# Values of two query chunks taken together in the second half of an attention kernel, with four tiles of transposed weights

## The chip, the cores and the metric

The kernel runs on one core of one Trainium2 chip. The core has five engines that run their own instruction streams in order and wait for each other by semaphores: TensorE (PE, matmuls; its weight loads are shown as PEld), VectorE (DVE), ScalarE (ACT), GpSimd (POOL) and SyncE (SP), which here only issues DMA transfers. Tiles live in SBUF (128 partitions) or PSUM (128 partitions, in banks of 512 float32, where matmuls put their results). The metric is the device time of one execution in microseconds (us); less is better. Runs of the kernel before: a median of 807.25 us of 3 (806.58 to 809.42).

## The reference

An attention of B = 4 batches, H = 8 heads, S = 576 positions and D = 64, with a bias that a small network of one hidden layer computes from the logarithm of the distance, and behind it an MLP with a squared ReLU on the 2304 tokens of 512 features:

```python
scores = scale * np.matmul(q, k.transpose(0, 1, 3, 2)) + bias
scores = scores - np.max(scores, axis=-1, keepdims=True)
attn = np.exp(scores)
attn = attn / (np.sum(attn, axis=-1, keepdims=True) + 1e-09)
x = np.matmul(attn, v)           # (B, H, S, D), then laid out as (B*S, H*D)
h = x @ w_in                     # 512 -> 2048
r = np.maximum(h, 0.0)
out = (r * r) @ w_out            # 2048 -> 512
```

## The kernel before, in words

The attention is cut into 80 units. A unit is one batch, one pair of heads (`hp`) and one chunk of queries (`ic`): four chunks of 128 queries and one last chunk (`TAIL`) of 64, in which both heads share one tile. Units 0 to 39 are batches 0 and 1; for them the bias is built beside the attention. Units 40 to 79 are batches 2 and 3, with the five chunks of one head pair in a row (`NA` = 40 is the border). This second half is where the change is.

A unit goes through three stages, each of them one or two units behind the one before in the loop over `s`:

- `scores(s)`: four matmuls (L428) into the tile `sp`, which is four banks of PSUM and exists once. DVE adds the bias and takes the row's maximum (L434, once for each head: the instructions `t,negm`, with a small one that reads `negm`), and ACT takes the exponential into `p` and the sums into `sums` (L439).
- `transposes(s - 2)`: PE transposes `p` into the PSUM tiles `pp` (eight 128x128 blocks, L477) and `pa` (the last keys of both heads, L480), and ACT copies them to the SBUF tile `pt` (L478, L481). There are two `pt` tiles, in the pool `att`.
- `values(s - 3)`: ten matmuls (L495) of `pt` with the values into the PSUM tile `px`, and one copy of `px` into the transposed output `xT` (L500), on DVE from unit 4 on.

When a head pair of a batch is complete, `normalise` (L448, L449) and `scale_x` multiply its part of `xT` by the inverse sums, which PE spreads over the partitions (`ra`, `rt`, L456, L463; DVE L466). All of `pp`, `pa`, `px`, `ra`, `rt` take turns in four banks with the tag `aux`.

Keys and queries of the second half come by SyncE's queue (L137 to L151) into the pool `kqb`, which takes the space of the first half's pool `kqa`, so that the first of these transfers waits for the last scores of unit 39. Behind them on the same queue come the weights. `load_w` (L172) brings 512 KB of `w_in` into one of two `stage` tiles, and `scan_w` takes its largest magnitude on DVE (L189, 16 scans from loop turn `SC` = 41 on, kept in the program's order). Once all 16 are through, one common scale is worked out (L215 to L218, and a matmul `pw`), and from turn `WB` = 53 on twelve of the weights are loaded again and split into two float16 parts (`split_in`): ACT takes a magnitude (L180), DVE works on the one tile `zw` (L183 to L186), POOL forms sums and differences (L238 to L240), ACT writes the high part (L227) and DVE the low part (L228) into `area`. The same four DVE operations on a tile `wa` begin the conversion of a weight of `w_out`; the first of these stand at the end of the attention, and more run in the MLP. The MLP's first matmuls (`ha`, L704) need the last `xT` of the batches, by way of the DVE multiplication L466 of the last head pair.

Nobody writes down the order of an engine's instructions: tiles are taken in turn from their pools, and a scheduler that simulates the engines' times sets the order in which each engine runs. The scans and the score matmuls are kept in program order. Where a change alters tiles or instructions, the order of others can change with it. These line numbers are those of the kernel before; in the kernel after, the value copy is L508, and L478, L481 and L495 are L479, L482 and L502.

Of the kernel before, what the change touches and what calls it, by code (L numbers as in the profile page):

```python
# [10 lines left out]
F32 = mybir.dt.float32  # L11
# [19 lines left out]
TAIL = 4  # L31
# [48 lines left out]
def attention_then_relu2_mlp(ctx: ExitStack, tc: tile.TileContext, q, k, v, cols, w_in, w_out, psi, xmat, dist, out):  # L80
    nc = tc.nc
    PE, DVE, ACT, POOL, SP = nc.tensor, nc.vector, nc.scalar, nc.gpsimd, nc.sync
# [5 lines left out]
    att = att_stack.enter_context(tc.tile_pool(name="att", bufs=1, side="right"))  # L88
# [37 lines left out]
    NA = len(units)  # L126
    units += [(b, hp, ic) for hp in range(HP) for b in range(AB, B) for ic in range(NIC)]
    NU = len(units)
    k1_t, v_t, q_t = {}, {}, {}
# [338 lines left out]
    def transposes(u):  # L468
        n = 2 if units[u][2] < TAIL else 1
        p = p_t.pop(u)  # L470
        b, hp, ic = units[u]
        pt = att.tile([128, 9, 128], F32, name="pt", tag="pt", bufs=2)
        for h in range(n):
            pp = ps.tile([128, 512], F32, name="pp", tag="aux", bufs=4)
            for c in range(4):
                k0 = h * (S + 64) + 128 * c
                PE.transpose(pp[:, 128 * c:128 * c + 128], p[:, k0:k0 + 128], ident)  # L477
            ACT.copy(pt[:, 4 * h:4 * h + 4], pp.rearrange("p (c m) -> p c m", c=4))  # L478
        pa = ps.tile([128, 512], F32, name="pa", tag="aux", bufs=4)  # L479
        PE.transpose(pa[:, :128], p[:, S - 64:S + 64], ident)  # L480
        ACT.copy(pt[:, 8], pa[:, :128])  # L481
        pt_t[u] = pt  # L482

    def values(u):
        b, hp, ic = units[u]
        pt, vt = pt_t.pop(u), v_t[b, hp]
        w = 64 if ic == TAIL else 128
        px = ps.tile([128, 512], F32, name="px", tag="aux", bufs=4)
        for c in range(5):
            for h in range(2):  # L490
                if c == 4:
                    src = pt[:, 8, 64 * h:64 * h + 64] if ic == TAIL else pt[:, 8, :w]
                else:
                    src = pt[:, c, 64 * h:64 * h + 64] if ic == TAIL else pt[:, 4 * h + c, :w]
                PE.matmul(px[64 * h:64 * h + 64, :w], lhsT=vt[:, c, h], rhs=src, start=(c == 0), stop=(c == 4))  # L495
        end = S if ic == TAIL else 128 * ic + 128
        if u < XC:
            ACT.copy(xT[b][:, hp, end - w:end], px[:, :w])
        else:
            DVE.tensor_copy(out=xT[b][:, hp, end - w:end], in_=px[:, :w])  # L500
# [376 lines left out]
```

## Time and profile before

One execution was recorded by the profiler. It took 803.41 us; its span from first to last instruction is 801.6 us.

| | us |
|---|---|
| median of 3 runs | 807.25 |
| profiled execution | 803.41 |
| span of it | 801.6 |
| PE busy | 731.9 (91%) |
| DVE busy | 546.0 (68%) |
| ACT busy | 453.8 (57%) |
| POOL busy | 272.8 (34%) |

The time is that of the whole program, and busy times are sums over it. The stages differ: the first half of the attention ends at about 208 us, the weights' scans at about 270, the attention at 402.7, and the MLP takes the rest. In a row of the timeline the last part in square brackets is the time for which the engine stood idle before it, and what it waited for; `x20` says that a row stands for 20 instructions. A float32 matmul of the program shows as two in the trace.

### The profile page before, as it was taken

What the parts mean: (1) busy time and instruction counts of PE and PEld (TensorE: products, weight loads), DVE (VectorE), ACT (ScalarE), POOL (GpSimd) and SP (SyncE); (2) the same over time, 40 slices, a digit from 0 to 9 for tenths busy, and PEclk for the clock granted to TensorE, in tenths of its full rate; (3) what the DMA queues carried; (4) which work ended last, traced back from release to release, by engine and by line L of the source; (5) the groups of instructions that cost most, each with busy time, mean ns of one, the idle gap of its engine ahead of it and who ended that gap; (6) DMA issues with size and microseconds to landing.
All of it is one profiled execution on the core that took longest, in us unless ns stands there. A gap on an engine that the chain in (4) does not pass through costs nothing.

```text
span 801.6 us, 17870 instructions
## 1 busy us (share of the span) xinstructions
PE 731.9 (91%) x7238; PEld 583.4 (73%) x7238; DVE 546.0 (68%) x1135; ACT 453.8 (57%) x924; POOL 272.8 (34%) x292
## 2 busy tenths in 40 slices
PE   6499999999988898988999899989999999999992
PEld 5457787777766676666678677767888888888881
DVE  7877888875457778887888968785654466445541
ACT  5767787777645468786865555575642233224320
POOL 1454323340001012141266645745451244223320
PEclk7979999999999999999999999999999999999997
DMA  7610000000475422211221132102020001000100
GB/s 207 188 57 17 3 16 3 2 3 5 125 276 196 159 81 88 84 54 54 80 90 70 66 119 104 55 1 79 1 79 1 1 1 54 1 1 2 53 2 26
DMA packets 27990, 50.14 MB, mean 63 GB/s; under 512 B 5252, under 2 KB 13444, under 8 KB 27908
## 3 DMA queue, kind: packets, MB, share of 16 engines
q1 hardware_dynamic: 27908, 49.01, 18.6%
q8 instruction: 57, 0.93, 0.5%
q14 instruction: 25, 0.20, 0.1%
HBM read 43.23 MB, written 5.77 MB: 61 GB/s over the span
## 4 chain that ended last, share of the span: by engine, by line
PE 53%; DVE 17%; ACT 8%; DMA 7%; issue 7%; POOL 4%; SPq 2%; POOLq 0%; DVEq 0%; ACTq 0%
PE y L753 16%; PE sp L428 8%; PE px L495 7%; PE ha L704 7%; PE hb L704 6%; PE pp L477 5%; DMA stage<-in_w_in 4%; PE bb L383 4%; DVE t L434 2%; ACT p L439 2%; DVE area L605 2%; ACT pt L478 1%; DVE zw L185 1%; DVE area L228 1%; DVE small L189 1%
## 5 line engine op out<-in xcount | busy, mean ns | idle before, releaser
L753 PE MATMUL y<-w,gh 128*128 128x512 f32 x576 | 176.7, 401 | 2.6 <-ACT gh L733 2.4
L704 PEld LDWEIGHTS <-area 128*128 128x128 f16 x1680 | 148.1, 99 | 42.2 <-issue 17.6
L439 ACT ACTIVATE p<-t,negm 128x576 f32<-128x576 f32 x144 | 111.4, 776 | 27.3 <-DVE negm L434 27.1
L434 DVE CUSTOM_DVE_ANT_0 t<-sp,area 128x576 f32<-128x576 f32 x144 | 104.0, 753 | 29.9 <-PE sp L428 24.8
L753 PEld LDWEIGHTS y<-w,gh 128*128 128x128 f32 x576 | 105.1, 190 | 23.9 <-ACT gh L733 3.8
L428 PE MATMUL sp<-k,q 64*128 64x288 f32 (+1 forms) x640 | 105.3, 441 | 15.4 <-DVE negm L434 7.6
L495 PE MATMUL px<-pt,v 128*64 128x128 f32 (+1 forms) x1600 | 99.2, 272 | 7.5 <-DVE xT L500 2.8
L753 PE MATMUL y<-w,gl 128*128 128x512 f32 x288 | 106.0, 395 | 0.0
L704 PE MATMUL ha<-area 128*128 128x256 f16 (+1 forms) x960 | 105.2, 263 | 0.5 <-DVE xT L466 0.5
L478 ACT COPY pt<-pp 128x512 f32<-128x512 f32 x144 | 80.4, 583 | 41.5 <-PE pp L477 41.4
L495 PEld LDWEIGHTS px<-pt,v 128*64 128x64 f32 x1600 | 81.5, 139 | 24.2 <-issue 9.5
L704 PE MATMUL hb<-area 128*128 128x256 f16 (+1 forms) x720 | 83.9, 270 | 8.0 <-DVE area L723 4.7
L477 PE MATMUL pp<-ident,p 128*128 128x128 f32 x576 | 84.7, 283 | 3.3 <-ACT p L439 2.5
L428 PEld LDWEIGHTS sp<-k,q 64*128 64x128 f32 (+1 forms) x640 | 55.2, 179 | 39.7 <-issue 14.0
L398 POOL TENSOR_TENSOR area<-bt,bt 128x256 f32<-128x256 f32 x72 | 53.5, 768 | 80.6 <-DVE bt L393 80.6
L477 PEld LDWEIGHTS pp<-ident,p 128*128 128x128 f32 x576 | 62.2, 142 | 21.3 <-issue 8.4
L383 PE MATMUL bb<-wmov,mask 128*128 128x64 f16 x1440 | 51.2, 197 | 13.7 <-DVE bt L404 11.0
L753 PEld LDWEIGHTS y<-w,gl 128*128 128x128 f32 x288 | 53.7, 188 | 11.9 <-DVE gl L734 0.7
L383 PEld LDWEIGHTS <-mask 128*128 128x128 f16 x1440 | 46.9, 100 | 20.7 <-DVE bt L404 11.8
L719 POOL TENSOR_TENSOR area<-area 128x512 f32<-128x512 f32 (+1 forms) x20 | 24.3, 1215 | 92.8 <-ACT area L718 83.9
L369 DVE TENSOR_TENSOR mask<-sdist,theta 128x1024 f16<-128x1024 f16 (+1 forms) x78 | 50.3, 677 | 7.9 <-PE bb L383 7.9
L733 ACT CAST gh<-area 128x512 fp32r<-128x512 f32 (+1 forms) x40 | 22.2, 574 | 44.0 <-DVE area L728 32.9
(146 smaller groups left out, 1024.2 us busy)
## 6 DMA issues: line engine op xcount, KB each, us to landing
stage<-in_w_in SPq DMA_DIRECT2D x32, 512.0 KB, 3.7
stage<-in_w_out SPq DMA_DIRECT2D x16, 512.0 KB, 3.5
v<-in_v SPq DMA_DIRECT2D x16, 320.0 KB, 3.7
out<-o SPq DMA_DIRECT2D x18, 256.0 KB, 2.0
q<-in_q SPq DMA_DIRECT2D x32, 128.0 KB, 2.9
k<-in_k SPq DMA_DIRECT2D x16, 160.0 KB, 3.5
k<-in_k SPq DMA_DIRECT2D x16, 144.0 KB, 3.5
xc<-in_xmat SPq DMA_DIRECT2D x5, 288.0 KB, 3.3
```

The source lines that it names most:

```text
L369: DVE.tensor_tensor(out=m[:, :, :w], in0=win, in1=th.to_broadcast([128, 8, w]), op=ALU.is_ge)
L383: PE.matmul(bb[:, 64 * (7 - r):64 * (8 - r)], lhsT=m[:, r], rhs=wmov[:, n], start=(n == 0), stop=(n == 1))
L398: POOL.tensor_tensor(out=dst, in0=tw, in1=sw, op=ALU.add)
L428: mm = PE.matmul(out_t[to, x, :HALF], lhsT=qt[rows, cols], rhs=kt[rows, k0:k0 + HALF], start=True, stop=True)
L434: DVE.tensor_tensor_reduce(out=t.rearrange("p (x n) -> p x n", x=2), in0=sp[:, :, :HALF], in1=bias.rearrange("p (x n) -> p x n", x=2), sca ...
L439: ACT.activation(out=p[:, S * n:S * n + S], in_=t, func=AF.Exp, bias=negm[:, n:n + 1], scale=-1.0, accum_out=sums[:, 2 * ic + n:2 * ic + n ...
L477: PE.transpose(pp[:, 128 * c:128 * c + 128], p[:, k0:k0 + 128], ident)
L478: ACT.copy(pt[:, 4 * h:4 * h + 4], pp.rearrange("p (c m) -> p c m", c=4))
L495: PE.matmul(px[64 * h:64 * h + 64, :w], lhsT=vt[:, c, h], rhs=src, start=(c == 0), stop=(c == 4))
L704: PE.matmul(h[:, s, :w], lhsT=a, rhs=x, start=(k == 0), stop=(k == 5))
L719: POOL.tensor_tensor(out=c[:, 2:4], in0=s[:, 1:3], in1=s[:, 0:4:3], op=ALU.subtract)
L753: PE.matmul(y, lhsT=a[:, slot, o:o + 128], rhs=x, start=((n, P) in firsts and f == 0 and m == 0), stop=((n, P) in lasts and f == 1 and m = ...
```

## The change

In units 40 to 79 the values of the chunks 0 and 1, and of 2 and 3, are taken together: for the first of a pair nothing is done, and for the second 20 matmuls are made, 128 columns of `px` for each unit, with one copy of 256 columns. The tail stays alone. To keep two units' transposed weights for that, `pt` tiles of the second half alternate, two units at a time, between the two tiles in `att` and two more in the pool `kqb`. A `pt` tile takes 4,608 bytes of a partition, so that 9,216 more are taken in `kqb`, and keys and queries lie elsewhere in it.

```diff
--- before.py
+++ after.py
@@ -469,7 +469,8 @@
         n = 2 if units[u][2] < TAIL else 1
         p = p_t.pop(u)
         b, hp, ic = units[u]
-        pt = att.tile([128, 9, 128], F32, name="pt", tag="pt", bufs=2)
+        pool = kq_p[-1] if u >= NA and u // 2 % 2 else att
+        pt = pool.tile([128, 9, 128], F32, name="pt", tag="pt", bufs=2)
         for h in range(n):
             pp = ps.tile([128, 512], F32, name="pp", tag="aux", bufs=4)
             for c in range(4):
@@ -482,17 +483,24 @@
         pt_t[u] = pt
 
     def values(u):
+
         b, hp, ic = units[u]
-        pt, vt = pt_t.pop(u), v_t[b, hp]
+        if u >= NA and ic in (0, 2):
+            return
+        vt = v_t[b, hp]
+        px = ps.tile([128, 512], F32, name="px", tag="aux", bufs=4)
         w = 64 if ic == TAIL else 128
-        px = ps.tile([128, 512], F32, name="px", tag="aux", bufs=4)
-        for c in range(5):
-            for h in range(2):
-                if c == 4:
-                    src = pt[:, 8, 64 * h:64 * h + 64] if ic == TAIL else pt[:, 8, :w]
-                else:
-                    src = pt[:, c, 64 * h:64 * h + 64] if ic == TAIL else pt[:, 4 * h + c, :w]
-                PE.matmul(px[64 * h:64 * h + 64, :w], lhsT=vt[:, c, h], rhs=src, start=(c == 0), stop=(c == 4))
+        us = [u - 1, u] if u >= NA and ic < TAIL else [u]
+        for n, m in enumerate(us):
+            pt = pt_t.pop(m)
+            for c in range(5):
+                for h in range(2):
+                    if c == 4:
+                        src = pt[:, 8, 64 * h:64 * h + 64] if ic == TAIL else pt[:, 8, :w]
+                    else:
+                        src = pt[:, c, 64 * h:64 * h + 64] if ic == TAIL else pt[:, 4 * h + c, :w]
+                    PE.matmul(px[64 * h:64 * h + 64, w * n:w * n + w], lhsT=vt[:, c, h], rhs=src, start=(c == 0), stop=(c == 4))
+        w *= len(us)
         end = S if ic == TAIL else 128 * ic + 128
         if u < XC:
             ACT.copy(xT[b][:, hp, end - w:end], px[:, :w])
```

The change moves instructions in places that the diff doesn't name. First SyncE, at the border of the halves: the last load of values, the keys of the first head pair of the second half (`k_4002`), and its queries (`q_4005`). In brackets are the semaphores that an instruction waits for; `PE_49` is the one that PE raises. Before:

```order
L143 DMA v<-in_v 128x640 [waits DMAHW2_49,PE_49]
L137 DMA k_4002<-in_k 64x576 [waits DMAHW3_49,PE_49]
L138 DMA k_4002<-in_k 64x640 [waits DMAHW4_49]
L150 DMA q_4005<-in_q 64x64 [waits DMAHW5_49]
L151 DMA q_4005<-in_q 64x4x128 [waits DMAHW6_49]
```

and after:

```order
L143 DMA v<-in_v 128x640 [waits DMAHW2_49,PE_49]
L137 DMA k_4002<-in_k 64x576 [waits DMAHW3_49]
L138 DMA k_4002<-in_k 64x640 [waits DMAHW4_49]
L150 DMA q_4005<-in_q 64x64 [waits DMAHW5_49,PE_49]
L151 DMA q_4005<-in_q 64x4x128 [waits DMAHW6_49]
```

The wait for PE stands at the first load of queries and no longer at the first load of keys.

Next DVE, from the second scan of a weight on (`reduce small<-stage`). Here `xT_76` and `xT_4000` are parts of the output of batches 0 and 2, and the pairs of `t,negm` and `negm` are the reductions of one head's scores. Before:

```order
L189 TENSOR_REDUCE small<-stage 128x1
L500 COPY xT_4000<-px 128x128
L189 TENSOR_REDUCE small<-stage 128x1
L434 ISA t,negm<-sp,area 128x576
L434 ISA negm 128x1
L434 ISA t,negm<-sp,area 128x576
L434 ISA negm 128x1
L466 TENSOR_TENSOR xT_76<-xT_76,ra 128x512
L466 TENSOR_TENSOR xT_76<-xT_76,rt 128x64
L189 TENSOR_REDUCE small<-stage 128x1
L189 TENSOR_REDUCE small<-xT_76 128x1
L500 COPY xT_4000<-px 128x128
```

and after:

```order
L189 TENSOR_REDUCE small<-stage 128x1
L466 TENSOR_TENSOR xT_76<-xT_76,ra 128x512
L466 TENSOR_TENSOR xT_76<-xT_76,rt 128x64
L189 TENSOR_REDUCE small<-xT_76 128x1
L434 ISA t,negm<-sp,area 128x576
L434 ISA negm 128x1
L434 ISA t,negm<-sp,area 128x576
L434 ISA negm 128x1
L189 TENSOR_REDUCE small<-stage 128x1 x2
L434 ISA t,negm<-sp,area 128x576
L434 ISA negm 128x1
L189 TENSOR_REDUCE small<-stage 128x1
```

The multiplications L466 have moved ahead of the reductions, the copy of `xT_4000` has gone further back, and the third and fourth scan stand side by side.

Last DVE again, at the end of the attention: the last reduction of scores (`t,negm<-sp,area`) is that of unit 79, `zw` belongs to the twelfth early split and `wa` to the first weight of `w_out`. Before:

```order
L186 SCALAR_TENSOR_TENSOR zw<-stage,zw 128x512
L434 ISA t,negm<-sp,area 128x576
L434 ISA negm 128x1
L189 TENSOR_REDUCE small<-xT_4000 128x1
L189 TENSOR_REDUCE small<-small 128x1
L183 TENSOR_SCALAR wa<-wa 128x512
L500 COPY xT_4001<-px 128x128
L184 TENSOR_SCALAR wa<-wa 128x512
L448 TENSOR_SCALAR sums<-sums 128x9
L185 SCALAR_TENSOR_TENSOR wa<-stage,wa 128x512
L449 RECIPROCAL sums<-sums 128x9
L500 COPY xT_4001<-px 128x128
```

and after:

```order
L434 ISA t,negm<-sp,area 128x576
L434 ISA negm 128x1
L183 TENSOR_SCALAR wa<-wa 128x512
L183 TENSOR_SCALAR zw<-zw 128x512
L184 TENSOR_SCALAR wa<-wa 128x512
L184 TENSOR_SCALAR zw<-zw 128x512
L185 SCALAR_TENSOR_TENSOR wa<-stage,wa 128x512
L185 SCALAR_TENSOR_TENSOR zw<-stage,zw 128x512
L448 TENSOR_SCALAR sums<-sums 128x9
L186 SCALAR_TENSOR_TENSOR wa<-stage,wa 128x512
L186 SCALAR_TENSOR_TENSOR zw<-stage,zw 128x512
L449 RECIPROCAL sums<-sums 128x9
```

The four operations on `zw`, the last of which stood ahead of the last reduction, now stand behind it, in turns with those on `wa`. In both kernels L228 follows, and behind it the multiplications L466 for which the MLP's first matmul waits.

## Rows read from the trace of the kernel before

**Rows 1.** Engines' busy time over the span, from the page

```profile
PE 731.9 (91%) x7238; PEld 583.4 (73%) x7238; DVE 546.0 (68%) x1135; ACT 453.8 (57%) x924; POOL 272.8 (34%) x292
```

**Rows 2.** By stretch: us, PE PEld DVE ACT POOL busy, PEclk, DMA, GB/s

```profile
279.80:393.40 113.60, 101.04 (x1091) 76.19 (x1090) 92.23 (x225) 88.19 (x201) 27.27 (x42) 0.98 0.21 70
```

**Rows 3.** SyncE's queue, second half's loads: start us, us, what, idle before

```profile
208.44 0.47 SPq L137 DMA_DIRECT2D k<-in_k  x1
...
209.59 0.60 SPq L150 DMA_DIRECT2D q<-in_q  x1
...
221.01 1.02 SPq L172 DMA_DIRECT2D stage<-in_w_in  x2
```

**Rows 4.** VectorE's timeline between scans 3 and 4, columns as in rows 3

```profile
233.04 0.75 DVE L434 CUSTOM_DVE_ANT_0 t<-sp,area 128x576 f32<-128x576 f32 x1
...
235.12 0.68 DVE L189 TENSOR_REDUCE small<-stage 128x1 f32<-128x512 f32 x1
```

**Rows 5.** Chain of waits ahead of 276 us: start us, us, what

```profile
264.24 4.95 DMA stage<-in_w_in
```

**Rows 6.** TensorE's timeline, scans and after, [idle before <-who ended it]

```profile
226.75 2.40 PE L495 MATMUL px<-pt,v 128*64 128x128 f32 x20 [2.81 <-DVE xT L500]
...
234.11 1.31 PE L495 MATMUL px<-pt,v 128*64 128x128 f32 x20 [0.16 <-ACT pt L478]
...
246.85 2.20 PE L495 MATMUL px<-pt,v 128*64 128x128 f32 x20 [2.06 <-DVE xT L466]
248.84 1.87 PE L456 MATMUL ra<-ident,sums 128*64 128x128 f32 x16
...
271.36 0.35 PE L198 MATMUL pw<-small,ones 128*128 128x1 f32 x2 [1.90 <-DVE small L218]
...
277.31 1.09 PE L477 MATMUL pp<-ident,p 128*128 128x128 f32 x8
...
278.44 0.80 PE L495 MATMUL px<-pt,v 128*64 128x64 f32 x20
...
279.76 1.24 PE L428 MATMUL sp<-k,q 64*128 64x288 f32 x8
```

**Rows 7.** TensorE's waits, 279.8 to 393.4: total us, times, longest

```profile
PE sp L428 <- DVE negm L434: 4.0, 5, 1.4
PE sp L428 <- DVE xT L500: 3.1, 3, 2.1
...
PE px L495 <- ACT pt L478: 1.2, 1, 1.2
```

**Rows 8.** Copies by shape: busy us, mean ns of one, idle before

```profile
L500 DVE COPY xT<-px 128x128 f32<-128x128 f32 x64 | 18.4, 287 | 10.5 <-PE px L495 10.0
...
L764 DVE COPY o<-y 128x256 f32<-128x256 f32 x2 | 0.8, 420 | 2.1 <-PE y L753 2.1
```

**Rows 9.** TensorE's timeline at the attention's end and in the MLP

```profile
393.40 1.19 PE L428 MATMUL sp<-k,q 64*64 64x288 f32 x8 [0.99 <-DVE negm L434]
...
402.68 2.78 PE L704 MATMUL ha<-area 128*128 128x256 f16 x24 [0.51 <-DVE xT L466]
...
410.90 2.14 PE L704 MATMUL hb<-area 128*128 128x256 f16 x18 [0.86 <-DVE c L723]
```

**Rows 10.** VectorE's timeline at the attention's end and in the MLP

```profile
399.82 1.15 DVE L228 SCALAR_TENSOR_TENSOR area<-zw,small,area 128x896 f16<-128x896 f32 x1
...
401.94 0.69 DVE L466 TENSOR_TENSOR xT<-xT,ra 128x512 f32<-128x512 f32 x1 [0.47 <-PE ra L456]
...
403.79 0.42 DVE L183 TENSOR_SCALAR wa<-wa 128x512 f32<-128x512 f32 x1
...
406.70 1.80 DVE L185 SCALAR_TENSOR_TENSOR wa<-stage,wa 128x512 int32<-128x512 int32 x1
```

**Rows 11.** GpSimd's timeline at the attention's end, first of three

```profile
396.01 0.73 POOL L238 TENSOR_TENSOR zw<-zw 128x256 f32<-128x256 f32 x1 [11.13 <-DVE zw L186]
```

**Rows 12.** ScalarE's timeline at the attention's end

```profile
398.38 1.06 ACT L227 ACTIVATE area<-zw,small 128x896 f16<-128x896 f32 x1
```

## The prediction

> **What bounds the kernel now.** I read the engines' busy line first: TensorE (PE) is busy for 731.9 of the 801.6 us of the span [rows 1], so time is lost only where PE stands idle or runs at its lower clock. The table by stretches then says where that is. The change touches units 40 to 79 alone, from 208 us on, so I cut there: loads and weight scans to 279.8, the plain second half to 393.4, its end to 402.7, and the MLP, which keeps its instructions. In the plain part PE is busy for 101.04 of 113.60 us, VectorE (DVE) for 92.23 [rows 2]: 12.6 us of idle PE is all that can be won there. Then I looked in each stretch for the wait that ends last. Up to 270 us it is the weights' DMA and the scans: the chain of waits goes through a stage load (4.95 us), the scan, the next load, and so on [rows 5]. In the plain part PE waits for reductions of scores on DVE (4.0), for value copies on DVE (3.1) and for tiles of transposed weights (1.2) [rows 7]. At the end it waits 0.51 for the last scaling of xT on DVE [rows 9].
>
> **What the copies are worth.** Over the 40 units, 32 copies of 128x128 become 16 of 128x256; eight of 128x64 stay. A 128x128 copy takes 287 ns, and the only 128x256 copies of this kernel out of PSUM, in the MLP, take 420 [rows 8]. So DVE saves 32 x 0.287 - 16 x 0.420 = 2.5 us. PE makes the same matmuls (the trace shows each matmul of float32 as two, so a unit's ten products stand as x20). The 2.5 us lie beside busy PE, except where PE waits for DVE. What the change does to the time is therefore mostly in what it moves.
>
> **A. The wait on the loads.** The new pool with its two more tiles shifts the keys' and queries' tiles, so that SyncE's wait for the last score of the first half stands at the first query load and no longer at the first key load. Two key issues go ahead of it, beside the wait that ended at 208.4. Before, the key issue began at 208.44 and the first query issue at 209.59; the first weight load went out at 221.01, behind all of them on the same queue [rows 3]. So every load behind comes 209.59 - 208.44 = 1.15 us earlier.
>
> **B. The scans.** DVE works in order. Scan 4 stands behind two reductions and two L466 multiplications that come after scan 3; from the first of them (233.04) to scan 4 (235.12) is 2.08 us [rows 4]. After the change those multiplications stand ahead of the next pair of reductions, and scans 3 and 4 stand side by side. With two stage buffers each later load waits for a scan, so this gain is passed on as far as DMA permits. A and B together: scan 16 is between 1.15 (A alone) and 4 us earlier (A, B and a little of the same kind further on). I take 3, near A + B = 3.2, since load 4 must itself have landed.
>
> **C. The turn at the scans' end.** In PE's new order the scores of units 51 and 52 stand back to back. The second waits for the reductions of unit 51, and these stand on DVE behind scans 15 and 16, two multiplications and the small reductions of the weights' scale. By durations that is some 4 us from scan 16's start, and PE has nothing in between: about 4.5 us idle, where before it waited 1.90 for the scale's matmul [rows 6]. An idle PE then runs slower here: after 2.81 us of waiting the next products took 2.40, after 2.06 us they took 2.20 and the matmuls behind them 1.87, against 1.31 for the same x20 at 234.11 [rows 6]. I price such a fall by those rows: (2.20 + 1.87) x (1 - 1.31 / 2.20) = 1.65 us. So of the 3 us only part is left when the score of unit 53 starts: I get 277.9 where it was 279.76 [rows 6], **-1.9**. But in the new order eight transposes, one more, and a tail's ten products of 64 columns stand behind that score that stood ahead of it: from 277.31 to 278.44, and 0.80 less some overlap from there [rows 6], **+1.85**. A, B and C give about nothing together.
>
> **D. The plain second half (units 53 to 79).** Four tiles of transposed weights take away the wait of 1.2 for such a tile; of the 3.1 that PE's scores stand behind value copies I take 0.8, as half the copies go and the rest are the longer ones. **-2.0**. Bounds: -6, if all of the 3.1 goes, the 1.2, and the rest of what DVE saves comes off the 4.0; +5 by the second rival.
>
> **E. The end.** Before, the last early split had its DVE part on zw done ahead of the last reduction, so that POOL, ScalarE (ACT) and L228 could work beside the last turns. In the new order these four zw operations stand behind the last reduction, each one behind its like of the weight wa, and the last L466 stands behind L228. The path from the start of the last score, step by step: the score 1.2 and its reduction 0.75, to 2.0; eight operations and two small ones on sums, where seven of the same kinds start from 403.79 to 406.70, 0.485 apart [rows 10], so 3.9 and 0.2, to 6.1; three POOL operations of up to 0.73 [rows 11], 2.0 with their overlap, to 8.1; ACT's L227, 1.06 [rows 12], to 9.2; L228, 1.15 [rows 10], to 10.3; two wa operations, a small copy and both L466 (0.69 the long one) [rows 10], 1.6, to 11.9. Before it was 402.68 - 393.40 = 9.28 [rows 9]: **+2.6**. The last score itself also comes later, since one more unit's products stand ahead of it (20 of the program's matmuls left behind it instead of 30): the 1.31 of x20 [rows 6] less its overlap, **+1.24**. PE is then idle for over 4 us in place of 0.51, and I add one fall of the clock, **+1.65** (0 to 1.65). In return the MLP's first wait for DVE, 0.86 at 410.90 [rows 9], should be gone, since some of its conversions' operations are then done: **-0.9**.
>
> **Sum.** -1.9 + 1.85 - 2.0 + 2.6 + 1.24 + 1.65 - 0.9 = +2.5. The profiled execution took 803.41 us (its span 801.6), so it would take 805.95. The median of the runs shown is 807.25, 3.84 above the profiled one; with that, 809.8.
>
> **The rivals.** First, **faster**: the scans' lead is kept and the end absorbs its stall. For it: the wait at C and the wait at E both depend on which of two engines is first, and where ACT or POOL is a little earlier than I have it, E is gone; 4.0 of the waits of D are on the very engine that is relieved. Against it: in the new order L466 stands behind L228. Price: D at -5 and E's +2.6 and +1.65 gone: 2.5 - 3 - 4.25 = -4.75, so 802.5. Chance 0.2.
>
> Second, **slower by uneven turns**: a pair's second unit now has 20 products and its first none. In the short turn PE has nine transposes (eight take 1.09 [rows 6], so 1.2 with the ninth) until the next score, and that score waits for two reductions, as there is one score tile; they take 0.75 each, 1.4 with their overlap [rows 4]. So PE loses at least 0.2 in each short turn, and 0.5 where DVE has one more operation ahead of them. With 11 pairs in units 53 to 79 that is +2 to +5.5; at +5 D turns from -2 to +5 and the time is 816.8. It decides from the point where another DVE operation stands ahead of the reductions in most short turns. Against it: the scheduler splits the 20 products around a score in places (17 and 3), and among even turns PE waited for reductions only five times [rows 7]. Chance 0.2.
>
> Third, **the shared bank**: the copy of a pair starts only when 20 products are through, where the first unit's copy could run beside the second's products. The trace has one place where products waited for a copy, 2.81 [rows 6], and PSUM has four such tiles in turn, so PE should have other work. Price from 16 x (0.420 - 0.287) = 2.1 to 16 x 1.31 = 21; at 5, with D's gain gone, 816.8. Chance 0.05. The Trainium skill, in "Perfetto Trace Analysis", section "Optimizing Tensor Performance", says in its part on matmuls that independent groups should rotate through PSUM banks so that the copy of one overlaps the next group's matmuls; by that rule this change goes the wrong way. That row of 2.81 is one case in 40 units, so the trace bears the rule out little here.
>
> Fourth, **nothing**: stalls at C and E do not grow and D is hidden: within 1 us of 807. Chance 0.1.
>
> **How the numbers follow.** My case has 0.45, with a range of its own of 806.5 to 813 (clock falls that do not come, D from -4 to +1). The range for 8 in 10, 802.5 to 816, takes in the faster rival's centre and most of the slower one. What a measurement of this kernel can tell from no change is 0.5%, 4.04 us: faster is under 803.2, slower over 811.3. Faster: 0.6 of the first rival, 0.12, the low tail of my case, 0.05, and of the fourth, 0.02: 0.19. Slower: three quarters of the second and third, 0.19, and the upper part of my case, 0.14: 0.33. The rest, 0.48, is no change.
>
> **What would show it.** A: the first stage load within 0.3 of 219.9. B: scan 16 at 265 to 268. C: an idle PE of over 3 us just ahead of the score of unit 52, with long products after it. D: the waits of PE on value copies and on pt below 3 us in all, and no row of waits on reductions above 6. E: over 3 us of idle PE ahead of the first ha matmul, released by L466. I am wrong if E's stall isn't there, or if waits on reductions in the plain part double: then the first or the second rival holds.

## The result and the profile after

The kernel with the pairs takes a median of 811.99 us in 20 runs (809.18 to 816.16); the kernel before takes 806.51 in the 20 beside it (803.76 to 810.0). The ratio is 1.0073, with a 95% interval of 1.0058 to 1.0088: slower by 0.73%, 5.5 us. The forecast was +2.5 us and 809.8; the time lies inside the range, and outside of what I called no change.

The profiled execution took 813.45 us, with a span of 811.7. The spans differ by 10.1 us, and not by 5.5, since the profiled execution of before is 3.1 us below its median and that of after 1.5 above. What follows divides the 10.1.

The busy line of the page, as [rows 1]:

```profile
PE 733.8 (90%) x7238; PEld 585.4 (72%) x7238; DVE 550.4 (68%) x1119; ACT 454.1 (56%) x924; POOL 273.0 (34%) x292
```

PE is busy for 1.9 us more than before, though its instructions are the same in number. By stretches (columns as in [rows 2]) the kernel before, from the score of unit 53 to that of unit 79, from there to the first ha, and the first 22 us of the MLP:

```profile
279.76:393.40 113.64, 101.08 (x1091) 76.23 (x1090) 92.27 (x225) 88.23 (x201) 27.27 (x42) 0.98 0.21 70
393.40:402.68 9.28, 8.58 (x123) 6.97 (x124) 8.74 (x23) 7.43 (x18) 4.39 (x6) 1.00 0.44 153
402.68:425.00 22.32, 21.05 (x160) 17.59 (x160) 18.51 (x30) 13.62 (x20) 15.38 (x11) 1.00 0.27 97
```

and the kernel after, with the end of the scans (from the score of unit 52) ahead of the same three:

```profile
271.18:280.51 9.33, 9.33 (x79) 7.62 (x80) 3.04 (x11) 3.11 (x9) 0.00 (x0) 0.64 0.01 2
280.51:394.65 114.14, 103.67 (x1139) 78.81 (x1138) 91.55 (x213) 87.79 (x200) 27.90 (x42) 0.99 0.21 65
394.65:407.96 13.31, 8.91 (x104) 7.58 (x103) 9.74 (x22) 7.94 (x16) 3.87 (x6) 0.87 0.30 106
407.96:430.00 22.04, 19.64 (x144) 16.26 (x144) 20.21 (x27) 13.09 (x18) 12.76 (x10) 0.92 0.30 97
```

The score of unit 53 starts at 280.51 instead of 279.76 (+0.75). The plain part takes 114.14 instead of 113.64 (+0.50), the end 13.31 instead of 9.28 (+4.03), and from the first ha to the end of the span it is 403.74 instead of 398.92 (+4.82). Together 10.1. So the plain part, where the copies are saved, is hardly moved; half of the loss is in the MLP, which the change does not touch.

The first of these terms depends on the execution that was traced. Ahead of unit 53, e2 and e3 below have the PE order of the kernel before. In their traces PE waits 2.38 and 2.33 for the scale's matmul, then has a granted clock of 0.61 and 0.70, and starts the score of unit 53 at 285.95 and 283.98. In the trace of before it waits 1.90, and the granted clock stays at 1.00.

SyncE's queue, which answers to [rows 3]:

```profile
207.23 0.59 SPq L138 DMA_DIRECT2D k<-in_k  x1
...
220.20 1.02 SPq L172 DMA_DIRECT2D stage<-in_w_in  x2
```

The keys go ahead of the wait and the first stage load goes out at 220.20, 0.81 us earlier. The end of the scans on PE, which answers to [rows 6]:

```profile
271.18 2.29 PE L428 MATMUL sp<-k,q 64*128 64x288 f32 x8 [4.69 <-DVE small L218]
...
275.09 3.77 PE L502 MATMUL px<-pt,v 128*64 128x128 f32 x40
...
280.51 1.23 PE L428 MATMUL sp<-k,q 64*128 64x288 f32 x6
```

PE waits 4.69 ahead of the score of unit 52. The score itself then takes 2.29 instead of 1.24, and 40 products take 3.77, where they take 2.40 at 392.32. The granted clock of this stretch is 0.64, so of its 9.33 busy us some 3.4 are the price of the low clock (9.33 x 0.36, an estimate that lets every duration follow the clock). The lead of the scans (the last begins at 267.29, where it was 269.21) is gone, and more.

PE's waits in the plain part, which answer to [rows 7]:

```profile
PE pp L478 <- ACT p L439: 4.5, 5, 1.4
PE sp L428 <- DVE negm L434: 1.9, 1, 1.9
...
PE sp L428 <- DVE xT L508: 0.8, 2, 0.5
...
PE px L502 <- ACT pt L479: 0.5, 1, 0.5
```

The waits for value copies fall from 3.1 to 0.8 and those of products for a pt tile from 1.2 to 0.5, as hoped; the wait of transposes for the exponentials takes part of their place, 4.5 where it was 2.5. The end on DVE, then on PE, which answer to [rows 9] and [rows 10]:

```profile
396.12 1.15 DVE L228 SCALAR_TENSOR_TENSOR area<-zw,small,area 128x896 f16<-128x896 f32 x1 [0.92 <-ACT area L227]
397.18 0.75 DVE L434 CUSTOM_DVE_ANT_0 t<-sp,area 128x576 f32<-128x576 f32 x1
...
401.13 0.68 DVE L186 SCALAR_TENSOR_TENSOR zw<-stage,zw 128x512 uint32<-128x512 uint32 x1
...
404.42 0.42 DVE L508 COPY xT<-px 128x256 f32<-128x256 f32 x1 [2.48 <-PE px L502]
404.88 1.15 DVE L228 SCALAR_TENSOR_TENSOR area<-zw,small,area 128x896 f16<-128x896 f32 x1
```

```profile
394.65 1.19 PE L428 MATMUL sp<-k,q 64*64 64x288 f32 x8
...
399.50 0.66 PE L478 MATMUL pp<-ident,p 128*128 128x128 f32 x4 [2.52 <-ACT p L439]
...
400.30 4.65 PE L502 MATMUL px<-pt,v 128*64 128x128 f32 x60
...
407.96 2.78 PE L712 MATMUL ha<-area 128*128 128x256 f16 x24 [1.87 <-DVE xT L466]
...
417.72 3.81 PE L712 MATMUL hb<-area 128*128 128x256 f16 x18 [2.40 <-DVE c L731]
```

The last reduction starts at 397.18, 2.5 after its score and not 1.2 as I had reckoned. It stands behind the L228 of the eleventh split, and that waited 0.92 for ACT's L227. (In the kernel before it starts 2.4 after its score, at 395.79.) Two paths lead from there to ha, and they are equally long. On the first come the operations on wa and zw in turns, then POOL, then ACT, whose L227 ends at 404.85, and the last L228 at 404.88. On the second PE waits 2.52 for the last exponential (the row at 399.50 is behind it) and then runs 60 products, those of the last pair and of the tail, in 4.65; e1 below runs the same 60 in 2.98. The copy of the pair, for which DVE stands idle for 2.48, ends at 404.84. Ha starts 1.87 after PE's last work.

In the MLP the next hb matmuls of PE wait for the two DVE operations on c, the halves of the first tile that DVE makes from hb. DVE in front of that wait, after the change:

```profile
412.73 1.64 DVE L186 SCALAR_TENSOR_TENSOR wa<-stage,wa 128x512 uint32<-128x512 uint32 x1
414.29 0.74 DVE L730 SCALAR_TENSOR_TENSOR c<-hb,small,c 128x512 f32<-128x512 f32 x1
415.62 1.38 DVE L183 TENSOR_SCALAR wa<-wa 128x512 f32<-128x512 f32 x1 [0.60 <-ACT wa L180]
416.93 0.74 DVE L731 SCALAR_TENSOR_TENSOR c<-hb,small,c 128x512 f32<-128x512 f32 x1
```

and before:

```profile
408.42 0.74 DVE L722 SCALAR_TENSOR_TENSOR c<-hb,small,c 128x512 f32<-128x512 f32 x1
409.08 1.10 DVE L186 SCALAR_TENSOR_TENSOR wa<-stage,wa 128x512 uint32<-128x512 uint32 x1
410.10 0.74 DVE L723 SCALAR_TENSOR_TENSOR c<-hb,small,c 128x512 f32<-128x512 f32 x1
```

Before, the last operation of the second of two conversions (L186) stands between the two halves of the first c (L722, L723), and the second half starts at 410.10, 7.4 us after ha. After, that operation stands ahead of the first half (L730, at 414.29, 6.3 us after ha and not 5.7). Between the halves stands an L183 of a third conversion, which waits 0.60 for ACT and takes 1.38. The second half (L731) starts at 416.93, 9.0 us after ha. PE waits 2.40 for it, and behind the wait 18 matmuls take 3.81, where they took 2.14 [rows 9].

### The profile page after: what moved, and what is told of

The parts are those of the page before. It is cut to its first block, busy times and chain, and to the rows that moved or that the text cites. A ratio compares the mean times of both kernels' runs of the same rounds, so it can differ in the third digit from the quotient of the medians.

```text
span 811.7 us, 17830 instructions
## 1 busy us (share of the span) xinstructions
PE 733.8 (90%) x7238; PEld 585.4 (72%) x7238; DVE 550.4 (68%) x1119; ACT 454.1 (56%) x924; POOL 273.0 (34%) x292
## 4 chain that ended last, share of the span: by engine, by line
PE 48%; DVE 21%; issue 8%; ACT 8%; DMA 6%; POOL 5%; SPq 1%; POOLq 0%; DVEq 0%; ACTq 0%
PE y L761 14%; PE sp L428 7%; PE ha L712 6%; PE px L502 6%; PE hb L712 5%; DMA stage<-in_w_in 5%; PE pp L478 4%; PE bb L383 4%; DVE t L434 3%; ACT p L439 2%; DVE zw L185 2%; DVE area L613 2%; DVE wa L185 1%; DVE wa L183 1%; ACT area L227 1%
## 5 line engine op out<-in xcount | busy, mean ns | idle before, releaser
L428 PE MATMUL sp<-k,q 64*128 64x288 f32 (+1 forms) x640 | 107.6, 446 | 16.1 <-DVE negm L434 8.0
L502 PEld LDWEIGHTS px<-pt,v 128*64 128x64 f32 x1600 | 84.6, 142 | 15.7 <-issue 6.9
L712 PE MATMUL hb<-area 128*128 128x256 f16 (+1 forms) x720 | 84.6, 271 | 10.5 <-DVE area L731 4.8
```

Source lines behind the costliest of these rows:

```text
L428: mm = PE.matmul(out_t[to, x, :HALF], lhsT=qt[rows, cols], rhs=kt[rows, k0:k0 + HALF], start=True, stop=True)
L502: PE.matmul(px[64 * h:64 * h + 64, w * n:w * n + w], lhsT=vt[:, c, h], rhs=src, start=(c == 0), stop=(c == 4))
L712: PE.matmul(h[:, s, :w], lhsT=a, rhs=x, start=(k == 0), stop=(k == 5))
```

## The experiments

All were timed in five rounds against the kernel before on the same chip. In these rounds the kernel before had medians from 805.83 to 807.40, so the ratios compare better than the medians. SC is the loop turn at which the scans begin, SN the number of turns over which they are spread, and WB the turn at which the early splits begin. The place of the last split is the number of DVE instructions from the last reduction of scores to the last zw operation of the twelfth early split (minus: ahead of it). The expectations count two equal instructions in a row as one, and so have 7, 21 and 16 where the table has 8, 22 and 17.

| run | values | SC, SN, WB | place of the last split | median us | ratio to before (95%) |
|---|---|---|---|---|---|
| before | single | 41, 10, 53 | -1 | 806.51 | 1 |
| after | pairs | 41, 10, 53 | +10 | 811.99 | 1.0073 (1.0058 to 1.0088) |
| e1 | pairs | 41, 10, 52 | -6 | 806.64 | 1.0002 (0.9982 to 1.0022) |
| e2 | single | 41, 10, 52 | +8 | 810.55 | 1.0040 (1.0015 to 1.0064) |
| e3 | single, four tiles | 41, 10, 53 | -1 | 804.64 | 0.9978 (0.9952 to 1.0004) |
| e4 | pairs | 42, 10, 53 | +10 | 806.05 | 0.9984 (0.9963 to 1.0006) |
| e5 | pairs, two banks | 41, 10, 53 | -2 | 805.97 | 0.9978 (0.9956 to 1.0001) |
| e6 | pairs | 41, 9, 51 | -6 | 808.35 | 1.0015 (0.9995 to 1.0035) |
| e7 | single, four tiles | 41, 9, 51 | -16 | 807.75 | 1.0014 (0.9994 to 1.0034) |
| e8 | single | 42, 10, 53 | +22 | 813.70 | 1.0085 (1.0055 to 1.0115) |
| e9 | pairs, two banks | 42, 10, 53 | -2 | 800.01 | 0.9932 (0.9907 to 0.9957) |
| e10 | pairs | 42, 10, 52 | -5 | 810.50 | 1.0061 (1.0039 to 1.0083) |
| e11 | single, four tiles | 42, 10, 52 | -17 | 799.48 | 0.9917 (0.9885 to 0.9949) |
| e12 | single | 42, 10, 52 | -17 | 802.84 | 0.9948 (0.9929 to 0.9967) |

The traced execution of each run, in us: the start of the reduction of unit 53 on DVE, then the time from it to the last reduction (unit 79), from there to the first ha, and from ha to the end of the span. Each row is one execution. Executions of the same kernel before differ by up to 9 us, so a difference of one or two us between two rows shows little.

| run | unit 53 | to unit 79 | to ha | to the end | span |
|---|---|---|---|---|---|
| before | 281.2 | 114.6 | 6.9 | 398.9 | 801.6 |
| after | 283.2 | 114.0 | 10.8 | 403.7 | 811.7 |
| e1 | 282.2 | 115.9 | 7.5 | 399.1 | 804.6 |
| e2 | 287.2 | 113.3 | 8.9 | 399.3 | 808.8 |
| e3 | 285.4 | 113.0 | 6.8 | 399.2 | 804.4 |
| e4 | 273.9 | 114.5 | 9.1 | 406.2 | 803.6 |
| e5 | 280.8 | 116.2 | 7.9 | 400.2 | 805.1 |
| e6 | 283.3 | 114.5 | 9.1 | 399.0 | 805.9 |
| e7 | 284.3 | 114.9 | 5.4 | 401.5 | 806.1 |
| e8 | 278.6 | 109.5 | 8.8 | 415.7 | 812.6 |
| e9 | 277.3 | 117.6 | 8.6 | 400.0 | 803.4 |
| e10 | 277.5 | 121.2 | 9.2 | 400.9 | 808.8 |
| e11 | 277.9 | 115.4 | 6.0 | 399.0 | 798.4 |
| e12 | 276.8 | 117.6 | 6.0 | 398.9 | 799.3 |

**The last split, in both kernels.** Theory: the late last split makes the end's stall and the MLP's. The rival: the pairs themselves cost. One number moves the splits by a turn, and the scheduler answers with an order of its own:

```diff
-WB = 53
+WB = 52
```

In the kernel after (e1):

> The kernel after with the early splits begun one turn earlier (WB = 52 for 53); by the new order the last split's DVE part on zw ends six DVE instructions ahead of the last reduction of scores instead of ten behind it, the scans' end with scores 51 and 52 back to back stays. My theory (the late last split makes the end's stall, 13.31 us from the last score to the first ha where it was 9.28, and its echo in the MLP's start): that stretch falls to under 10 us, PE waits under 1.0 for the last L466, and the median goes from 812.0 to 803 to 807. Rival (uneven turns or the shared bank cost in the plain part): the end heals but the median stays at 810 to 813.

and in the kernel before (e2):

> The kernel before, without pairs, with the same WB = 52. Its own new order puts the last split's DVE part on zw seven instructions behind the last reduction of scores, as the kernel after has it (ten). My theory: it shows the same end, over 12 us from the last score to the first ha, and a median of 809 to 813, with no pair of units in it. Rival (the loss belongs to the pairs): within 2 us of the kernel before, 805 to 808.

Measured: 806.64 with pairs and 810.55 without. The last products, the first ha and the first wait for c in e1's trace:

```profile
400.90 2.98 PE L502 MATMUL px<-pt,v 128*64 128x128 f32 x60
...
405.55 2.78 PE L712 MATMUL ha<-area 128*128 128x256 f16 x24 [0.53 <-DVE xT L466]
...
413.78 2.14 PE L712 MATMUL hb<-area 128*128 128x256 f16 x18 [0.86 <-DVE c L731]
```

and the first ha in e2's:

```profile
409.47 2.78 PE L704 MATMUL ha<-area 128*128 128x256 f16 x24 [1.72 <-DVE xT L466]
```

With the last split ahead of the last reduction, PE waits 0.53 and 0.86 as before [rows 9], and from ha to the end it takes 399.1. The loss is gone with the pairs still there. With the last split behind it, the kernel without pairs waits 1.72 and loses 4 us. Both medians are those of my theory. Of the lengths, e1's end from the last score to ha is 8.9 as expected (under 10), and e2's 11.0, less than the 12 that I asked for and 1.8 more than before.

E2 bears the theory out less than its median says. Of the 7.2 us between its trace and that of before, 2.0 are at the end; 6.1 are there ahead of unit 53, where the last split plays no part, and 4.2 of such a delay stand in e3's trace too, in a kernel that loses nothing. Among the kernels without pairs the place of the last split shows at the end all the same: 8.9 and 8.8 from the last reduction to ha where it stands behind (e2, e8), 5.4 to 6.9 where it stands ahead (before, e3, e7, e11, e12). In e2 the MLP stays at 399.3, so the stall at the end and the longer MLP are two things; the kernel after has both.

With pairs the place is not all. E6 and e10 have the last split ahead of the last reduction, as e1 has, and still take 9.1 and 9.2 to ha. In both PE waits over 2 us for the last exponential and then runs the last 60 products slowly, as in the kernel after; e10:

```profile
401.46 0.66 PE L478 MATMUL pp<-ident,p 128*128 128x128 f32 x4 [2.43 <-ACT p L439]
...
402.35 4.51 PE L502 MATMUL px<-pt,v 128*64 128x128 f32 x60
```

In e1 that wait is 1.17, and the products take 2.98. Without pairs 20 products of an earlier unit stand in this place, and PE waits only 0.43 to 0.46 (e7, e11, e12). So the pairs have a price of their own at the end, and whether it is paid depends on how late the last exponential comes.

**The tiles alone (e3).** The kernel before with the change of the first hunk, the place of the `pt` tiles, and nothing else:

```diff
-        pt = att.tile([128, 9, 128], F32, name="pt", tag="pt", bufs=2)
+        pool = kq_p[-1] if u >= NA and u // 2 % 2 else att
+        pt = pool.tile([128, 9, 128], F32, name="pt", tag="pt", bufs=2)
```

> Only the four pt tiles (two of them in kqb), values and copies as before; DVE's order at the end is that of the kernel before. My theory: the earlier loads give 1 us and the wait for a pt tile 1.2 at most; 804 to 807. Rival (the place of the tiles, keys and queries costs): 809 or more.

804.64, ratio 0.9978 with an interval that just reaches 1: no loss, a gain of 1.8 us that isn't clear. The place of the tiles is not the cause.

**The scans, with pairs (e4) and without (e8).** The scans start a turn later:

```diff
-SC = 41
+SC = 42
```

> The kernel after with the scans begun one turn later (SC = 42): by the new order the values of a pair stand between the scores of the units at the scans' end, no longer back to back, and the end of the attention is as in the kernel after. My theory: PE's wait of 4.69 there falls under 2.5, which is worth 1 to 3 us of the loss, and the end's stall stays: 809 to 812. Rival (the stall at the scans' end makes the loss): 805 to 807.

> The kernel before with SC = 42, the control to the kernel after with the same. By its new order the last split's DVE part stands 21 instructions behind the last reduction of scores. My theory: the scans' end is passed with one unit more done, as there, but the late split costs 3 to 6 at the end: 806 to 811. Rival (the gain of 6 us there is the scans' turn alone): 800 to 803.

e4 gave 806.05, which is the rival's number, and e8 813.70, slower than I thought. In e4 the wait of 4.69 is gone and the reduction of unit 53 starts 6.2 us after the last scan, where it is 15.9 in the kernel after. Part of that is one more unit done by then, and that part is large. E10, e11 and e12 below, with the scans in the same turn, wait even longer than the kernel after; e11:

```profile
275.61 2.29 PE L428 MATMUL sp<-k,q 64*128 64x288 f32 x8 [6.35 <-DVE small L189]
```

Still they reach the reduction of unit 53 at 276.8 to 277.9, where it is 283.2 in the kernel after and 273.9 in e4. So the later turn of the scans seems to be worth more than the end of the stall (these three also begin the splits a turn earlier); what the stall alone costs was not separated. PE at e4's end and the MLP's start:

```profile
397.45 2.78 PE L712 MATMUL ha<-area 128*128 128x256 f16 x24 [0.17 <-DVE xT L508]
...
403.81 2.78 PE L712 MATMUL ha<-area 128*128 128x256 f16 x24 [1.62 <-ACT s L726]
409.66 2.14 PE L712 MATMUL hb<-area 128*128 128x256 f16 x18 [3.07 <-DVE c L731]
```

Ha starts 10.5 us earlier than in the kernel after, and 5.2 earlier than in the kernel before, but from it to the end it is 406.2 instead of 398.9: the MLP's first products wait 1.62 and 3.07. Its start has the order of the kernel after, with a third conversion between the halves of c. In e8 the MLP takes 415.7 from a ha at 396.94. An attention that ends early wins little in these two. That the conversions and the first c stand in each other's way there is read from the waits; no run moved them alone.

**Two banks (e5).** The pairs' turns stay, each unit has a px tile and a copy of its own:

```diff
-        px = ps.tile([128, 512], F32, name="px", tag="aux", bufs=4)
...
         for n, m in enumerate(us):
             pt = pt_t.pop(m)
+            px = ps.tile([128, 512], F32, name="px", tag="aux", bufs=4)
+            pxs.append(px)
```

> The kernel after with the pairs' turns as they are, but each unit's products in a px tile (bank) of its own and two copies of 128x128 in place of one of 128x256. Its new order has the scans' end as in the kernel after (scores 51 and 52 back to back) and the last split's DVE part two instructions ahead of the last reduction. My theory (the late last split makes most of the loss, the copy itself little): the end takes under 11 us, the MLP starts without long waits, 805 to 809. Rival (pairs' uneven turns cost): 810 to 813, as the kernel after. If the shared bank costs, it is below 804.

805.97, as expected, though PE still waits 1.63 for the first c. It does not show the price of the shared bank, for the order of the end changed too: the last split stands ahead again.

**Pairs against single values with the same numbers.** First with the scans ended and the splits begun earlier, with pairs (e6) and with the tiles alone (e7):

```diff
-WB = 53
+WB = 51
...
-SN = 10
+SN = 9
```

> The kernel after with the scans ended one turn earlier (SN = 9) and the early splits begun two turns earlier (WB = 51): by the new order a pair's values stand between the scores at the scans' end, and the last split's DVE part ends six instructions ahead of the last reduction. My theory: neither the wait of 4.69 nor the end's stall is there; ha begins before 402, and the MLP gives part of it back as in the run with the scans moved, where it took 406.2 from ha to the end instead of 399: 801 to 805. Rival: as the kernel before, 806 to 808.

> The four pt tiles alone, values and copies as before, with the same SN = 9 and WB = 51, so that it differs from the mended kernel after by the pairs alone. If pairing gains (2.5 us of DVE time and 2 us of PE's waits, as I forecast for the plain part), it is 1 to 3 us slower than that one; rival (uneven turns cost): 1 to 5 us faster than it.

808.35 and 807.75: my numbers for e6 are missed, as its PE waits 4.03 at the scans' end, and the two medians are equal within the noise. In the traces they are equal by two differences that cancel: the end takes 9.1 in e6 and 5.4 in e7 (the last exponential, above), and the MLP 399.0 and 401.5. E7's MLP has the order of the kernel before at its start, and PE still waits 2.34 for c. Then the scans a turn later, with two banks (e9, which keeps WB = 53), and with the splits a turn earlier too, pairs (e10), tiles alone (e11) and the kernel before (e12):

```diff
-WB = 53
+WB = 52
...
-SC = 41
+SC = 42
```

> The pairs' turns with two banks and two copies, and SC = 42. By its order a pair's values stand between the scores at the scans' end, the last split's DVE part ends two instructions ahead of the last reduction, and at the MLP's start two conversions run in turns on DVE with the first c between their last operations, as in the kernel before. My theory (DVE's order at the end and at the MLP's start, and the scans' turn, are the whole difference): first ha before 400, 399 from it to the end of the span, 798 to 803. Rival (the conversions set the MLP whenever the attention ends, as in the kernel after with the scans moved): 805 to 807.

> The kernel after with SC = 42 and WB = 52: pairs with one copy, the last split's DVE part five instructions ahead of the last reduction, and the MLP's start in the order of the kernel before. My theory: first ha before 400, 399 from it to the end, 798 to 803, that is 3 to 8 less than the kernel after with SC = 42 alone, which has the other order at the MLP's start and took 406.2 from ha to the end. Rival: 805 to 807, as that one.

> The four tiles alone, single values and copies, with SC = 42 and WB = 52: last split 16 instructions ahead of the last reduction, the MLP's start in the order of the kernel before. It differs from the pairs with the same numbers by the pairs alone. If pairing is worth the 2 us of waits that I took for the plain part, it is 1 to 3 slower than them; by what the first two such runs gave (808.35 with pairs, 807.75 without) it is within 1.5.

> The kernel before with SC = 42 and WB = 52 and nothing else: two pt tiles, single values and copies; its order at the scans' end, the attention's end and the MLP's start is that of the four tiles alone with the same numbers, which took 799.48. My theory (the order makes the difference, the tiles little): 799 to 803. Rival (the two more tiles are what gains): 804 or more.

e9's median and e12 came out as the theory had it (in e9's profiled execution, 5 us above its median, ha begins at 403.4 and not before 400). e10 and e11 did not: 810.50 and 799.48, with the last split ahead of the last reduction in both, 11 us apart and the other way than a gain of the pairs. In the source e10 differs from e11 by the pairs alone, and both come to the reduction of unit 53 at about the same time (277.50 and 277.94). Of the 10.4 us between their traces 5.8 are in the plain part, 3.2 between the last reduction and ha, and 1.8 in the MLP, where PE waits 2.35 for the first c (0.88 in e11), although DVE has the order of the kernel before there:

```profile
417.66 2.14 PE L712 MATMUL hb<-area 128*128 128x256 f16 x18 [2.35 <-DVE c L731]
```

The plain part of e10, then of e11, cut here from the reduction of unit 53 to that of unit 79 (columns as in [rows 2]):

```profile
277.50:398.70 121.20, 107.28 (x1152) 80.72 (x1153) 96.86 (x224) 90.36 (x205) 29.23 (x45) 0.98 0.22 70
```

```profile
277.94:393.37 115.43, 106.35 (x1155) 80.05 (x1155) 96.69 (x239) 91.82 (x206) 29.33 (x45) 0.99 0.24 76
```

PE is idle for 13.9 us with pairs and 9.1 without. Its transposes wait for exponentials nine times, 6.8 us in all, with pairs and four times, 3.6, without; its scores wait for reductions 3.8 and 2.0. One short turn, the first, shows how such a wait comes about. PE and DVE with pairs:

```profile
282.60 1.24 PE L428 MATMUL sp<-k,q 64*128 64x288 f32 x8
...
285.05 1.10 PE L478 MATMUL pp<-ident,p 128*128 128x128 f32 x8
289.65 2.29 PE L428 MATMUL sp<-k,q 64*128 64x288 f32 x8 [3.50 <-DVE negm L434]
```

```profile
285.81 0.43 DVE L183 TENSOR_SCALAR zw<-zw 128x512 f32<-128x512 f32 x1
...
287.46 0.69 DVE L186 SCALAR_TENSOR_TENSOR zw<-stage,zw 128x512 uint32<-128x512 uint32 x1
288.07 0.75 DVE L434 CUSTOM_DVE_ANT_0 t<-sp,area 128x576 f32<-128x576 f32 x1
```

and without:

```profile
283.45 1.24 PE L428 MATMUL sp<-k,q 64*128 64x288 f32 x8
284.62 1.31 PE L496 MATMUL px<-pt,v 128*64 128x128 f32 x20
...
287.58 1.24 PE L428 MATMUL sp<-k,q 64*128 64x288 f32 x8
```

```profile
284.80 0.75 DVE L434 CUSTOM_DVE_ANT_0 t<-sp,area 128x576 f32<-128x576 f32 x1
```

In e10 the score at 282.60 is followed by no products but only by sums and transposes; its two reductions stand on DVE behind the four zw operations of a split and start at 288.07. PE has nothing until 289.65, 3.50 us, and then runs the score in 2.29 instead of 1.24. In e11 the reductions start at 284.80, 1.35 after the score, and PE works on the products meanwhile. This is my second rival, with the condition I gave it: other DVE work ahead of the reductions in a short turn. The other short turns were not followed one by one. It costs by the order that the scheduler happens to find: e6's stretch from unit 53 to unit 79 takes 114.5, and that of e7, without pairs, 114.9.

e9, e11 and e12 are faster than the kernel before by 0.5 to 0.8%; e11 (0.9917, 0.9885 to 0.9949) and e12 need no pairs. Between these two the intervals overlap, so what the two more tiles give is not settled.

Against the kernel before with the same numbers, pairs (with the four tiles) lose 5.5 us in the change itself, gain 3.9 (e1, e2) and 7.6 (e4, e8), and lose 7.7 (e10, e12). So the sign goes with the numbers, which change the order, and not with the pairs alone; but the lowest median with pairs and one copy, 806.05, is above that of single values with two tiles, 802.84.

## Why the prediction was right, and where it was not

Range and sign held, and the likeliest case was the right one in its places: no gain from the copies, a lost lead at the scans, a stall at the end. Its sizes were not right, and the chance of no change (0.48) stood above that of slower (0.33), which is what came. The sum was for the traced executions, and there it is short by 7.6: +2.5 for 10.1. That the median came within 2.2 of 809.8 is partly luck, since the traced execution of before is one of its faster ones (3.1 below the median) and that of after one of its slower (1.5 above).

- A and B. Right: the first stage load at 220.20 (I said 219.9) and the last scan at 267.29 (265 to 268).
- C. The wait was right (4.69, I said 4.5), its price was not: the score of unit 53 came at 280.51 and not 277.9. I priced the clock's fall by two rows, 1.65; at 0.64 over 9.33 us it is 3.4. e4, without the stall, is 5.9 us below the kernel after in the median, but with the scans' turn in it, and e10 to e12 gain by that turn with a longer stall. What the stall alone costs stays open.
- D. The plain part with its 3.1 us of moved work takes 0.50 more; I had -2.0 + 1.85 + 1.24 = +1.1. PE's idle time there fell from 12.56 to 10.47, 2.1 us as I said. But that did not lower the time: in three comparisons with the four tiles alone and equal numbers, pairs gain nothing (e6, e7) or lose (after and e3, e10 and e11).
- E. The stall is there, +4.03 for my +2.6. Of the missing 1.4, 1.3 are that the last reduction began 2.5 and not 1.2 after its score, behind the L228 of the split before; from the reduction on the path takes 10.8, and I had 10.7. I had read the order of the last split and not who stood ahead of the last reduction. The sign that I gave, over 3 us of idle PE just ahead of ha, is not met: there it is 1.87, and 2.52 came earlier, ahead of the last transposes. The fall of the clock that I added (1.65) came with that wait: 60 products in 4.65 where e1 takes 2.98. It did not add to the path, since DVE's L228 waited as long for ACT. The counts in the forecast are off too: 30 of the program's products and not 20 stand behind the last score (60 rows), where there were 40 and not 30; the difference, which the sum uses, is right.
- The failed step is the credit of 0.9 for the MLP's start, together with its one fall of the clock, +1.65: I reckoned +0.75, and it is +4.82. I took it that operations done earlier would shorten the MLP. Instead the first c comes later behind ha: the whole second conversion now stands ahead of it, and a third begins between its halves. So PE waits 2.40 where it waited 0.86 (+1.5), works on at a low clock (+1.7), and waits 1.7 more at 450 to 453 for the split of x (L613), for which it did not wait before. e1, e2 and e3, whose MLP starts in the old order, take 399.1 to 399.3 from ha to the end; e4, in the new order, 406.2. The order is not the whole cause: e7 and e10 start in the old one, wait 2.34 and 2.35 for the first c, and take 401.5 and 400.9. There an L184 ahead of c takes 1.50, beside an operation of GpSimd, where it takes 0.42 in e1. What sets the length of these operations stays open.

The first rival (faster) is refuted for this kernel; the mechanism that it needed, an end without a stall, gives back the 5.4 us in e1, no more. The second did not decide in the plain part, where the waits for reductions fell from 4.0 to 1.9; e10 has its cost there (5.8 us more than e11), and in the kernel after, e6 and e10 the pairs leave PE without work during the last exponential. The third, the shared bank, stays open: no run changed the bank and nothing else, as each changed the order too. That the loss at the end and in the MLP goes with the order, and not with the pairs as such, rests on e1 alone; e2 repeats the end's part, 2 us of it. That it is the place of the last split, and not something else that moved with it, is not shown: it was not tried to move the last split's instructions by hand in an order that is otherwise kept.

## What to carry to other kernels

Where a scheduler sets the order, price a change by the order of the new kernel, at the places where one stage ends and the next begins, and go on through the first work of the next stage: here 4.8 of 10.1 us were lost in a stage that was not changed. Before a structure is judged, move one number that shifts the order in both kernels: a run of each gave 806.6 for pairs and 810.6 for single values, the reverse of the first comparison. And before a wait is blamed, look whether a faster kernel has it too: e11 has the longest stall at the scans' end and the lowest median. Pairing leaves every second turn short, so PE has less to do while it waits for reductions and exponentials; in the three comparisons here with the four tiles alone and equal numbers they did not gain.

## What the runs showed of the hardware

- Single executions of the same kernel before spread from 802.68 to 811.97 us in 35 runs, more than the whole effect; a difference of two profiled executions (10.1) can be twice that of the medians (5.5).
- A wait of PE can cost more than its length, and does not always. After 4.69 us of it the granted clock stood at 0.64 over the next 9.33 us, which adds an estimated 3.4 us; after 2.40 us in the MLP the next 18 matmuls took 3.81, 1.67 more. But after 3.07 us in e4 and 2.35 us in e10 the same 18 took 2.14, as after a short wait.
- The same DVE operation has two durations: L186 takes 0.68 at 401.13, where GpSimd does nothing, and 1.64 at 412.73, beside two operations of GpSimd that are long too (one of the same shape took 1.27 a little later):

```profile
412.11 1.71 POOL L727 TENSOR_TENSOR c<-s 128x512 f32<-128x512 f32 x1
413.78 1.72 POOL L728 TENSOR_TENSOR c<-s 128x512 f32<-128x512 f32 x1
...
419.90 1.27 POOL L727 TENSOR_TENSOR area<-area 128x512 f32<-128x512 f32 x1 [3.18 <-ACT area L726]
```

  The Trainium skill, in "SBUF — State Buffer", section "Terms", has VectorE and GpSimd share a pair of ports that one of them holds for a whole instruction. These rows agree with that, in that both take longer side by side; that it is the ports was not tested. It makes a conversion that the order puts ahead of c dearer than its durations in the attention say.
